# Banded attention with a bilinear FFN on one core: weighted sums of two head pairs moved, scores of a third joined to them, output banks in another order

## The chip, the core and the metric

The kernel runs on one core of one Trainium2 chip. Its engines work side by side and meet at semaphores: TensorE (PE; PEld is its weight load), VectorE (DVE), ScalarE (ACT), GpSimd (POOL) and SyncE (SP), which here only issues DMAs. The metric is the device time of one launch in microseconds (us), as a median over runs; lower is better.

## The reference

For 8 sequences (here "batches") of 576 tokens with 8 heads of 64:

```
scores = q k^T / 8 - slope[h] * |i - j|      (only 0 <= i - j < 128, elsewhere -1e9)
attn   = softmax(scores);  x = attn v         (x: 4608 tokens x 512)
out    = ((x w_a) * (x w_b)) w_out            (d_ff = 1536)
```

Inputs and output are f32. The kernel computes the large products in f16 with each operand split into a high and a low half (three matmuls for one product), so that PE does three times the plain number of matmuls.

## The kernel before

**Two streams on PE.** The main stream is the FFN: per batch an `up` phase (x times w_a and w_b, their product) and a `down` phase (times w_out). From batch 1 on, PE's order is the written order (`manual_schedule` for PE alone). ACT, DVE, POOL and SP are ordered by a planner that simulates the program: whatever is ready first in that simulation goes first, with ties by written order and by priority; `tc.issue_after(x)` keeps an instruction behind x. The order of each queue is then fixed, and each engine works through its own in turn.

**A step** of the main stream is six matmuls of 288 columns (function `terms`, or two f of `down`). For batches 4 to 6, `up` has 84 steps in two interleaved lanes (`up_fast`): each lane owns one `ch` bank, which ACT reads after its first, and third step (L1158, L1170) and DVE after its fifth and seventh (L1181, L1193); the lane's `p` steps use one of the two side banks ef0 and ef1 (read at L1165, L1176, L1186). The next use of a bank waits for that read. Batches 1 to 3 do all, six or two of the twelve f in a plainer way (`up_plain`, read at L1084 and L1086).

**The side stream** is the attention of the next batches, generator `attention()`. It goes pair by pair (two heads, p = 0 to 3 in a batch). `weave` and `Pace` set how far it may go: its values `yield i + v/7` are places, and one pair takes 24 steps of a `down` or 42 of an `up`. During `up` of batch b it is at pairs p = 2 and p = 3 of the batch b + 1; during `down` at p = 0 and p = 1 of the batch after. The parts of a pair are:

- `score_pair(o, 0)`, `score_pair(o, 1)`: 64x64 matmuls of q and k into two banks each, then DVE's bias and minimum (L508) and ACT's exponential (L509); the second bank's DVE and ACT work is a function `rest` that is called later.
- `normalize`: probabilities in f16, high half by ACT (L547), low half by DVE (L548), into the one buffer `packed` (tile phl).
- `transpose_probs`: one DMA transpose on SP's queue from `packed` into the one buffer pT (L558).
- `split_v`: v in two f16 halves (vhl, two buffers). `pv_phase(0)`, `pv_phase(1)`: 36 and 30 to 36 matmuls of 64x64 that form x; between them DVE reads one column (`mid`, L677), after them ACT copies x out (`keep_x`, L567) and squares it.
- `split` and `lay_out`: q and k of the next pair in two halves (`qkh` by ACT L459, `qkl` by DVE L464) and copied across partitions (tile qst, one buffer, four DMAs on SP); `load`: the DMAs of the pair after (one buffer qk, free after L464).

Score and x banks, and two small sums, come in turn from a ring of four banks (place "at"). The pair p = 1 is not transposed in its own turn: its transpose and its products with v come in p = 2, behind those of p = 0 (held in `late`).

**Banks of the main stream.** `places["bank"]` is an endless cycle over ef0, ef1 and the two `ch` buffers; `up_plain` takes four an f, `down` takes eight a batch (dn_ps, read at L1243) and `hidden_scale` two. The cycle goes on from batch to batch without a restart.

Of the kernel before, what the change touches and what calls it, by code (L numbers as in the profile page):

```python
# [88 lines left out]
def attention_then_bilinear_ffn(ctx: ExitStack, tc: tile.TileContext, qT, kT, vP, w_a, w_b, w_out, rel, slopes2, outT):  # L89
# [12 lines left out]
    def share_banks():  # L102

        places["ef"] = three[:2]
        places["bank"] = cycle(three[:2] + ((ps_ch, "ch"),) * 2)
        places["at"] = cycle(((ps_at, "at"),) * 3 + three[2:])

# [733 lines left out]
    def attention():  # L841
# [36 lines left out]
        for i in range(n + 1):  # L878
# [6 lines left out]
            if p == 3 and b > 1:  # L885
                pv_phase(1, late.p, st, late)
                transpose_probs(prev)
            if two == 2:
                rest = score_pair(o, 0, nxt.ready if p == 1 and nxt else None)
                yield i + 0.5 / 7  # L890
                rest()
            elif o:
                scores(o, 0)
# [18 lines left out]
            if p == 2 and b > 1:  # L912
                pv_phase(0, late.p, st, late)
                split(nxt)
            elif p == 2:
                pv(late.p, st, late, late.vhl)
                transpose_probs(prev)
                split(nxt)
# [5 lines left out]
            if p == 0 and prev and prev.b > 1:  # L924
                yield i + 2.3 / 7
                pv_phase(0, prev.p, st, prev)
            yield i + 3 / 7
            if two == 2:
# [3 lines left out]
                elif p == 3:  # L932
                    pv_phase(0, prev.p, st, prev)
                    yield i + 3.7 / 7
                if p == 0 and prev.b > 1 or p == 3:
                    pv_phase(1, prev.p, st, prev)
                elif p == 2:
                    pv_phase(1, late.p, st, late)
                    transpose_probs(prev)
                rest = score_pair(o, 1)  # L940
                yield i + (3.5 if p in (1, 2) or p == 0 and prev.b > 1 else 4.2 if p == 3 else 4) / 7
# [3 lines left out]
                yield i + (4.2 if p == 3 else 4) / 7  # L945
# [27 lines left out]
            if o:  # L973
                with behind():
                    normalize(o)
            if p == 0 and b == 1:
# [8 lines left out]
            if p == 2 and b > 1:  # L985
                pv_phase(0, prev.p, st, prev)
            elif p == 2:
                pv(prev.p, st, prev, prev.vhl)
            if p == 1 or p == 2 and b > 1:
                late = prev  # L990
            elif o:
                transpose_probs(o)
            prev, o = o, nxt
# [392 lines left out]
    def batch(b):  # L1386
# [10 lines left out]
        weave(att.along(up(states[b], h, plain, fast, seven), n_up, NPAIR * b + 4), *sides[0])  # L1397
        if seven:
# [10 lines left out]
    share_banks()  # L1409
    with tc.manual_schedule(engines={mybir.EngineType.PE}):  # L1410
# [42 lines left out]
```

## Time and profile before

| | |
|---|---|
| median of 3 runs | 989.89 us (988.83 to 992.11) |
| profiled execution | 988.87 us, span 987.1 us, granted clock 0.998 of full |
| PE busy | 945.2 us (96%), 10312 matmuls |
| DVE, ACT, POOL busy | 721.7 us (73%), 636.0 us (64%), 261.0 us (26%) |

A busy PE is a modelled figure: a matmul of 288 columns is shown as 286 ns, though the next one starts 0.12 us after it. Where PE is fed, a step therefore starts 0.73 to 0.74 us after the step before; a later start is a loss, a little larger than the idle time that a row shows.

### The profile page before, as it was taken

The numbers are of one execution on the slowest core, as the hardware profiler recorded it, in microseconds if no ns is written. First come the engines' busy times: TensorE is split into PE (matmuls) and PEld (weight loads), VectorE is DVE, ScalarE is ACT, GpSimd is POOL, SyncE is SP. The second block draws the span as 40 slices with busy tenths as digits, with TensorE's granted clock in tenths as the row PEclk, the third lists the DMA queues.
The fourth block names the chain that finished last, engine by engine and source line by source line (L and its number), as shares of the span: only waits on it lengthen the run. The fifth ranks groups of instructions, "written<-read, shape, count | busy, mean of one in ns | idle before, by whom it ended". The sixth has DMA issues, their size and how long they took to land.

```text
span 987.1 us, 25870 instructions
## 1 busy us (share of the span) xinstructions
PE 945.2 (96%) x10312; PEld 732.2 (74%) x10313; DVE 721.7 (73%) x2028; ACT 636.0 (64%) x1725; POOL 261.0 (26%) x307
## 2 busy tenths in 40 slices
PE   8989999989989999998999999999899999999998
PEld 6657777767767777776777777777677777777776
DVE  6999997577878758766886676767677685589860
ACT  6878788576676667766766766767567765434531
POOL 1211132045455123640533012321134012221110
PEclk9999999999999999999999999999999999999999
DMA  9372845513335232453135342363314521200001
GB/s 343 136 270 95 268 92 127 150 37 75 73 88 149 50 46 56 101 144 72 37 72 136 75 72 42 81 151 75 78 42 92 149 48 37 42 31 13 1 7 43
DMA packets 136152, 91.15 MB, mean 92 GB/s; under 512 B 101600, under 2 KB 122208, under 8 KB 135008
## 3 DMA queue, kind: packets, MB, share of 16 engines
q1 hardware_dynamic: 126528, 79.97, 33.0%
q10 hardware_dynamic: 9504, 9.54, 3.0%
q8 instruction: 80, 1.31, 0.6%
q14 instruction: 40, 0.33, 0.1%
HBM read 48.33 MB, written 9.44 MB: 59 GB/s over the span
## 4 chain that ended last, share of the span: by engine, by line
PE 59%; DVE 12%; ACT 12%; DMA 11%; issue 3%; POOL 2%; SPq 1%; ACTq 0%; DVEq 0%; POOLq 0%
PE ch L1073 13%; PE up_ps L1073 12%; PE p L1073 10%; PE dn_ps L1238 10%; DMA pT<-phl 6%; PE x_ps L674 3%; PE dn_ps L1035 2%; ACT t L509 2%; DMA qk<-in_kT 2%; DVE t L508 2%; DMA v<-in_vP 2%; PE dch L1263 2%; ACT phl L547 2%; DVE xr L589 2%; PE d L1263 1%
## 5 line engine op out<-in xcount | busy, mean ns | idle before, releaser
L1073 PEld LDWEIGHTS <-wup 128*128 128x128 f16 x3072 | 295.7, 98 | 101.5 <-issue 26.1
L1238 PE MATMUL dn_ps<-h,wdn 128*128 128x288 f16 x1728 | 218.9, 286 | 2.9 <-DVE row L1186 1.1
L1073 PE MATMUL up_ps<-xr,wup 128*128 128x288 f16 x1536 | 197.2, 286 | 8.2 <-ACT xr L1084 4.6
L1238 PEld LDWEIGHTS <-wdn 128*128 128x128 f16 x1728 | 165.7, 98 | 47.4 <-issue 3.5
L1073 PEld LDWEIGHTS <-wsum 128*128 128x128 f16 x1152 | 111.5, 98 | 39.1 <-issue 10.0
L1188 POOL TENSOR_TENSOR xr<-xr,row 128x288 f32<-128x288 f32 x64 | 60.0, 938 | 299.4 <-DVE row L1186 272.4
L509 ACT ACTIVATE t<-t,mn 128x192 f32<-128x192 f32 (+2 forms) x252 | 107.5, 431 | 29.6 <-DVE mn L508 29.6
L1073 PE MATMUL ch<-xr,wup 128*128 128x288 f16 x768 | 115.0, 286 | 9.2 <-DVE xr L1193 7.4
L1073 PE MATMUL ch<-xr,wsum 128*128 128x288 f16 x768 | 111.3, 286 | 7.7 <-ACT xr L1158 7.6
L1073 PE MATMUL p<-xr,wup 128*128 128x288 f16 x768 | 115.1, 286 | 0.4 <-ACT xr L1176 0.4
L548 DVE SCALAR_TENSOR_TENSOR phl<-t,rin,phl 128x192 f16<-128x192 f32 (+2 forms) x252 | 100.5, 444 | 15.5 <-ACT phl L547 14.6
L547 ACT ACTIVATE phl<-t,rin 128x192 f16<-128x192 f32 (+2 forms) x252 | 89.2, 429 | 26.2 <-DMA pT<-phl 13.1
L1065 ACT CAST h<-xr 128x576 f16<-128x576 f32 x84 | 56.2, 669 | 49.2 <-DVE xr L1086 18.5
L508 DVE CUSTOM_DVE_ANT_0 t<-sc_ps,bias,neg 128x192 f32<-128x192 f32 (+2 forms) x216 | 73.3, 390 | 9.8 <-PE sc_ps L525 9.6
L1066 DVE TENSOR_TENSOR h<-xr,h 128x576 f16<-128x576 f32 x78 | 60.8, 779 | 25.8 <-ACT h L1065 24.8
L589 DVE TENSOR_TENSOR xr<-v,xr 128x576 f16<-128x576 f32 x52 | 49.8, 968 | 26.7 <-ACT xr L588 26.4
L483 POOL TENSOR_SCALAR bias<-rel_sb,ninv,sl_sb 128x192 f32<-128x192 f32 x24 | 26.9, 1122 | 152.9 <-DVE mn L508 125.7
L1170 ACT ACTIVATE row<-ch,g 128x288 f32<-128x288 f32 x64 | 31.8, 497 | 52.6 <-PE ch L1073 51.1
L1073 PE MATMUL p<-xr,wsum 128*128 128x288 f16 x384 | 57.6, 286 | 0.1
L588 ACT CAST xr<-v 128x576 f16<-128x576 f32 x52 | 34.9, 673 | 21.3 <-POOL v L607 16.6
L509 ACT ACTIVATION_READ_ACCUMULATOR t<-t,mn 128x1 f32 x252 | 48.5, 193 | 0.0
L583 POOL TENSOR_TENSOR xq<-xq,sq 128x576 bf16<-128x576 bf16 x21 | 30.7, 1462 | 53.0 <-ACT sq L582 52.8
(200 smaller groups left out, 1553.4 us busy)
## 6 DMA issues: line engine op xcount, KB each, us to landing
v<-in_vP SPq DMA_DIRECT2D x8, 1280.0 KB, 6.2
qk<-in_qT SPq DMA_DIRECT2D x28, 288.0 KB, 3.9
qk<-in_kT SPq DMA_DIRECT2D x28, 288.0 KB, 4.6
out<-row ACTq DMA_DIRECT2D x56, 144.0 KB, 2.2
wdn<-in_w_a SPq DMA_DIRECT2D x12, 512.0 KB, 5.0
wdn<-in_w_b SPq DMA_DIRECT2D x12, 512.0 KB, 6.0
wdn<-in_w_out SPq DMA_DIRECT2D x12, 512.0 KB, 6.0
qst<-qkh SPq DMA_DIRECT2D x24, 80.0 KB, 2.3
```

The costliest lines, as they stand in the source:

```text
L508: beside[1] = vec.tensor_tensor_reduce(out=t[:, c:c + w], in0=ps[:, c:c + w], in1=o.bias[:, WIN - w:WIN], scale=-0.125 if o.b == 1 else o. ...
L509: beside[0] = act.activation(t[:, c:c + w], t[:, c:c + w], AF.Exp, bias=o.mn[:, n:n + 1], scale=-1.0, accum_out=o.sm[:, n:n + 1])
L547: beside[0] = last_phl[0] = act.activation(to[:, 0, pc:pc + w], e, AF.Copy, scale=s)
L548: beside[1] = vec.scalar_tensor_tensor(out=to[:, 1, pc:pc + w], in0=e, scalar=s, in1=to[:, 0, pc:pc + w], op0=ALU.mult, op1=ALU.subtract)
L588: act.copy(xs[:, n, 0, :, :], src)
L589: vec.tensor_tensor(out=xs[:, n, 1, :, :], in0=src, in1=xs[:, n, 0, :, :], op=ALU.subtract)
L1065: act.copy(h[:, f, :, 0, :], hid)
L1066: eng.tensor_tensor(out=h[:, f, :, 1, :], in0=hid, in1=h[:, f, :, 0, :], op=ALU.subtract)
L1073: pe.matmul(ps[:, 0:HT], w[:, wi, k, :], xs[:, b, xi, k, :], start=(first and n == 0), stop=(last and n == len(ks) - 1), skip_group_check= ...
L1170: last_read[0] = last_main[0] = act.activation(mid, ch, AF.Copy, scale=st.g)
L1188: pool.tensor_tensor(out=x0, in0=x0, in1=mid, op=ALU.mult)
L1238: pe.matmul(ps[:, 0:HT], wdn[:, f, wi, e * P:(e + 1) * P], h[:, f, t, hi, :], start=(m == 0 and n == 0), stop=(m == NF - 1 and n == 2))
```

## The change

It has four parts. In pair p = 2 (`b > 1`) the second half of the products of pair 0 with v, the transpose of pair 1 and the second scores come at place 2.5/7 in place of 3/7, and the second scores' `rest` at 3/7 in place of 3.5/7. The products of pair 1 with v come at 5.5/7 and 6/7 of p = 2, in place of 6/7 and of the start of p = 3; the transpose of pair 2 and the first scores of pair 3 follow them at 6/7, so the first scores of p = 3 leave the start of p = 3 and only their `rest` stays there, without the half place between. In p = 3 the products of pair 2 with v come at 2.3/7 and 3/7 (before 3/7 and 3.7/7), the second scores with them, their `rest` at 3.5/7 (before 4.2/7). Last, the cycle of banks is restarted before every `down`, in the order side bank, `ch`, other side bank, `ch`, with the first side bank by the number of fast f.

```diff
     def share_banks():
         places["ef"] = three[:2]
-        places["bank"] = cycle(three[:2] + ((ps_ch, "ch"),) * 2)
         places["at"] = cycle(((ps_at, "at"),) * 3 + three[2:])
+
+    def down_banks(n):
+
+        a = max(n, 1) % 2
+        places["bank"] = cycle((three[a], (ps_ch, "ch"), three[1 - a], (ps_ch, "ch")))
...
             if p == 3 and b > 1:
-                pv_phase(1, late.p, st, late)
-                transpose_probs(prev)
-            if two == 2:
+                rest()
+            elif two == 2:
                 rest = score_pair(o, 0, nxt.ready if p == 1 and nxt else None)
                 yield i + 0.5 / 7
                 rest()
...
             if p == 2 and b > 1:
                 pv_phase(0, late.p, st, late)
                 split(nxt)
+                yield i + 2.5 / 7
+                pv_phase(1, late.p, st, late)
+                transpose_probs(prev)
+                rest = score_pair(o, 1)
             elif p == 2:
...
-            if p == 0 and prev and prev.b > 1:
+            if prev and prev.b > 1 and p in (0, 3):
                 yield i + 2.3 / 7
                 pv_phase(0, prev.p, st, prev)
             yield i + 3 / 7
@@
-                elif p == 3:
-                    pv_phase(0, prev.p, st, prev)
-                    yield i + 3.7 / 7
-                if p == 0 and prev.b > 1 or p == 3:
+                elif p in (0, 3):
                     pv_phase(1, prev.p, st, prev)
-                elif p == 2:
-                    pv_phase(1, late.p, st, late)
-                    transpose_probs(prev)
-                rest = score_pair(o, 1)
-                yield i + (3.5 if p in (1, 2) or p == 0 and prev.b > 1 else 4.2 if p == 3 else 4) / 7
+                if p != 2:
+                    rest = score_pair(o, 1)
+                    yield i + (4 if p == 0 and prev.b == 1 else 3.5) / 7
                 rest()
                 if p == 3 and nxt:
                     low_qk(nxt, beside[1])
-                yield i + (4.2 if p == 3 else 4) / 7
+                yield i + 4 / 7
...
+            if p == 2 and b > 1:
+                yield i + 5.5 / 7
+                pv_phase(0, prev.p, st, prev)
...
             if p == 2 and b > 1:
-                pv_phase(0, prev.p, st, prev)
+                pv_phase(1, prev.p, st, prev)
             elif p == 2:
                 pv(prev.p, st, prev, prev.vhl)
-            if p == 1 or p == 2 and b > 1:
+            if p == 1:
                 late = prev
             elif o:
                 transpose_probs(o)
+            if p == 2 and b > 1:
+                rest = score_pair(nxt, 0)
             prev, o = o, nxt
             yield i + 1
...
         weave(att.along(up(states[b], h, plain, fast, seven), n_up, NPAIR * b + 4), *sides[0])
+        down_banks(len(fast) // 2)
         if seven:
...
     share_banks()
+    down_banks(0)
     with tc.manual_schedule(engines={mybir.EngineType.PE}):
```

## Rows read from the trace of the kernel before

**Rows 1.** The page's chain that ended last, by line, share of the span.

```profile
PE ch L1073 13%; PE up_ps L1073 12%; PE p L1073 10%; PE dn_ps L1238 10%; DMA pT<-phl 6%; PE x_ps L674 3%; PE dn_ps L1035 2%; ACT t L509 2%; DMA qk<-in_kT 2%; DVE t L508 2%; DMA v<-in_vP 2%; PE dch L1263 2%; ACT phl L547 2%; DVE xr L589 2%; PE d L1263 1%
```

**Rows 2.** Waits of PE, whole span: us in total, times, longest us.

```profile
PE ch L1073 <- ACT xr L1158: 7.6, 9, 2.3
PE ch L1073 <- DVE xr L1193: 7.4, 9, 2.0
PE up_ps L1073 <- ACT xr L1084: 4.6, 4, 1.8
...
PE ch L1073 <- ACT row L1170: 1.9, 2, 1.2
...
PE sc_ps L525 <- ACT v L567: 1.4, 3, 0.7
...
PE dn_ps L1238 <- DVE row L1186: 1.1, 1, 1.1
```

**Rows 3.** PE in time, batch 4: start, us, line, tiles, count, idle before and releaser.

```profile
579.70 0.90 PE L1073 MATMUL ch<-xr,wsum 128*128 128x288 f16 x6
582.49 0.90 PE L1073 MATMUL ch<-xr,wsum 128*128 128x288 f16 x6 [1.89 <-ACT xr L1158]
```

**Rows 4.** ACT in time, batch 4, ahead of that start.

```profile
577.56 0.67 ACT L1065 CAST h<-xr 128x576 f16<-128x576 f32 x1 [0.31 <-DVE xr L1193]
580.48 1.68 ACT L547 ACTIVATE phl<-t,rin 128x192 f16<-128x192 f32 x5 [2.24 <-DMA pT<-phl]
582.06 0.38 ACT L1158 COPY xr<-ch 128x288 f32<-128x288 f32 x1
```

**Rows 5.** Waits of ACT on that transfer, 280 to 860 us.

```profile
ACT phl L547 <- DMA pT<-phl: 13.1, 6, 3.1
```

**Rows 6.** PE's waits of this kind in batch 6 (782 to 854 us).

```profile
PE ch L1073 <- ACT xr L1158: 0.4, 1, 0.4
```

**Rows 7.** SP's queue in time: batch 2, then batch 4.

```profile
342.09 3.91 SPq L558 DMA_TRANSPOSE pT<-phl  x1
...
571.04 0.60 SPq L431 DMA_DIRECT2D qk<-in_qT  x1
...
572.39 5.18 SPq L558 DMA_TRANSPOSE pT<-phl  x1
```

**Rows 8.** ACT in time, batch 2: the wait after the first of these transposes.

```profile
348.89 1.68 ACT L547 ACTIVATE phl<-t,rin 128x192 f16<-128x192 f32 x5 [1.37 <-DMA pT<-phl]
```

**Rows 9.** PE in time, batch 4, start of pair 3.

```profile
597.23 0.90 PE L1073 MATMUL ch<-xr,wup 128*128 128x288 f16 x6 [0.77 <-DVE xr L1193]
597.96 0.90 PE L1073 MATMUL p<-xr,wup 128*128 128x288 f16 x6
...
601.18 0.65 PE L1073 MATMUL ch<-xr,wsum 128*128 128x288 f16 x4 [0.85 <-ACT xr L1158]
```

**Rows 10.** ACT in time, batch 4, before and at the start of pair 3.

```profile
587.83 0.50 ACT L1170 ACTIVATE row<-ch,g 128x288 f32<-128x288 f32 x1 [1.28 <-PE ch L1073]
...
598.72 1.17 ACT L442 ACTIVATE qkl<-qk 128x1152 bf16<-128x1152 f32 x1
...
600.75 0.38 ACT L1158 COPY xr<-ch 128x288 f32<-128x288 f32 x1
```

**Rows 11.** PE in time, batch 4: the second scores of pair 2.

```profile
570.58 0.69 PE L674 MATMUL x_ps<-pT,vhl 64*64 64x128 f16 x30
...
571.72 0.27 PE L525 MATMUL sc_ps<-qkh,qst 64*64 64x192 f16 x2 [0.36 <-ACT v L567]
```

**Rows 12.** ACT in time around those scores.

```profile
568.31 1.26 ACT L459 ACTIVATE qkh<-qk,own 128x1152 f16<-128x1152 f32 x1 [0.90 <-DVE own L457]
...
571.23 0.71 ACT L567 ACTIVATE v<-x_ps 128x320 f32<-128x320 f32 x2
```

**Rows 13.** PE in time, from up to down of batch 3.

```profile
512.35 0.90 PE L1073 MATMUL ch<-xr,wsum 128*128 128x288 f16 x6
514.37 0.65 PE L1238 MATMUL dn_ps<-h,wdn 128*128 128x288 f16 x4 [1.12 <-DVE row L1186]
```

## The prediction

> **What bounds the kernel now.** I read the busy table first: PE is busy 96% of the span, so only what PE loses can be won. Then the chain that ended last [rows 1]: its long links are PE's own steps, but one DMA stands among them, the transpose into pT, with 6% of the span. Then PE's waits [rows 2]: the two largest kinds are a `ch` bank that ACT (L1158, 7.6 us in 9 waits) or DVE (L1193, 7.4 us in 9) has not yet read. Last, I followed PE's steps in time, batch by batch. The `down` phases from batch 2 on run without a wait of note; the losses sit in the `up` phases, where pairs 2 and 3 are worked in. There the same few places recur, and the change touches four of them. A loss is counted from start to start: a step takes 0.735 us when it is fed (597.23 to 597.96, [rows 9]), so the step of [rows 3] that starts at 579.70 should be followed at 580.44, is followed at 582.49, and loses 2.05 us where the row shows 1.89 us of idle time. I add 0.16 us to each wait for that.
>
> **What does not change.** No matmul, ACT, DVE or DMA instruction is added or removed. A stretch of 64x64 matmuls between main steps has a switch in and out; there are seven such stretches in an `up` before, at steps 1, 13, 19, 37, 43, 61 and 65 of 84 (place v/7 comes after step 6v, rounded down, plus 1; 42 more for pair 3), and seven after, at steps 1, 13, 16, 34, 37, 56 and 61. So that part costs nothing, because the first scores of pair 3 go along with the products they stood beside before. PE's order is written out; the orders on ACT, DVE and SP are the planner's, and that is where the doubt lies.
>
> **A, the banks.** At the end of `up` of batch 3 the first dn_ps lies in the side bank whose last reader is the last but one step of the later lane: it starts at 514.37 in place of 512.35 + 0.735 = 513.09 and loses 1.28 us [rows 13]. With five fast pairs of f the new cycle begins with ef1, which the earlier lane left some steps before. In batches 4 to 6 the cycle happened to begin well, and in batch 1 the order is a ring of four as before, so nothing is won there. Between 0 (something else is late there) and 1.3, I take -1.2 us.
>
> **B, the transpose of pair 1.** This is the largest term. In pair 2, ACT's first probability op (L547) must wait until the transpose has read `packed`; it waits 2.24 us until 580.48, and L1158 stands behind it on ACT's queue until 582.06 [rows 4]. PE's step waits for just that read [rows 3]. So 2.05 us of PE are lost to a transfer. ACT has six such waits, 13.1 us together [rows 5]: five lie at this place (batches 2 to 6), the sixth in a `down`, where PE does not feel it. PE's losses by it are 2.3 + 0.16 in batch 5, 2.0 + 0.16 in batch 3 (the longest of the two kinds, [rows 2]; there the late read is DVE's, which waits for ACT), 2.05 in batch 4, 0.4 + 0.16 in batch 6 [rows 6], about nothing in batch 2 (plain steps, more slack). Sum 7.2 us. The transpose waits for the last product of pair 0; with these three steps sooner it can be issued 3 x 0.735 = 2.2 us sooner, against waits of 1.4 to 3 us [rows 5, 8]. The `rest` of the second scores comes three steps sooner too, so ACT arrives a little sooner, which eats some of that. Bounds: 0, if SP issues it no sooner (below), and -7.2; I take -6.0.
>
> A rule bears on this term. On SP the transpose stands behind the two loads of q and k (571.04 first, transpose 572.39, [rows 7]) and is 8.1 us from issue to ACT's release (580.48, [rows 4]); in batch 2 without loads just ahead it is 342.09 to 348.89, 6.8 us [rows 7, 8]. If the transpose now goes first, I count 6.8 us. The Trainium skill, "DMA: Bandwidth & Descriptors", section "Issuing engines are not separate DMA queues", says that all DMAs run on the same 16 DMA engines and interleave, so that loads issued right behind would stretch the transpose as loads ahead of it do. The two rows agree with some stretch; by the rule the term would be some 1.3 us smaller in each of batches 3 to 5, so -2.1 in place of -6.0.
>
> **C, the start of pair 3.** Before, ACT and DVE get there at once the x copies of pair 1, v's halves, five minima and exponentials and the squares of the next pair: L1158 runs at 600.75, behind the squares at 598.72 [rows 10], and PE loses 0.77 + 0.16 and 0.85 + 0.16 us within six steps [rows 9]. There are seven such losses: two each in batches 4 and 5, one each in batches 2, 3 and 6; with 0.93 to 1.02 us each, 6.7 us. After the change the products and the first three minima fall at step 37, where ACT had idle time (1.28 us before L1170 at 587.83, [rows 10]), and only `rest` and the squares stay at step 43. The work is the same, spread over six more steps. Not all of it is won, since after step 37 a lane's L1193 follows just as it did after step 43, one step later. Bounds 0 and -6.7; I take -4.0.
>
> **D, the second scores behind the x copies.** The ring of four banks gives the second scores' second bank the place of the first x bank, so PE waits in the middle of a stretch: 571.72 for L567, which starts at 571.23 [rows 11, 12]. There are three such waits, 0.7 us longest [rows 2]; with the start to start loss 2.1 us. At the new place, three steps after the first products and the small sum for the next pair, ACT's qkh (L459, 568.31 to 569.57) is just under way when the products end at about 569.1 (570.58 + 0.69 - 3 x 0.735). L567 then starts at about 569.6, the bank is free at 570.0, and PE loses 1.05 us, in batches 3 to 6, with 0.5 in batch 2: 4.7 in place of 2.1. Bounds: 0 more (L567 goes before qkh), and 2.2 more in each of five batches if L567 starts no sooner than today; I take +2.6.
>
> **E, a denser ACT after it.** qkh (1.26), the x copies (0.71), then exponentials now fall into the three steps in which the lanes' own reads were alone. No row of before has that crowd at this step; the nearest is C's, 0.93 to 1.02 us lost for a crowd. From nothing to 1.0 in each of five batches, I take half: +2.5. The wait for `mid` between the two halves of products has now three steps in place of six; a read of one column with 2.2 us of room costs nothing unless DVE is that far behind. Waits of the plain batches (L1084, 4.6 us, [rows 2]) lie mostly in the early steps of pair 2, which don't move: 0.
>
> **Sum.** -1.2 - 6.0 - 4.0 + 2.6 + 2.5 = -6.1 us. Against the profiled execution of 988.87 us that is 982.8; the median of the runs is 1.0 us above that execution, so I predict 983.7 us for the median.
>
> **The rivals.**
>
> 1. *The transpose goes no sooner.* The planner issues SP's queue in its own order; the loads wait for L464, the last reader of their one buffer, and today start at 571.04 [rows 7], beside the products' end (570.58 + 0.69, [rows 11]). If it still puts them ahead of the transpose, the transpose is issued at 572.4 as before, and B is 0. For: the loads stand first today. Against: L464 does not move, so they would be ready some 2 us after the products now. The sum is -1.2 - 4.0 + 2.6 + 2.5 = -0.1: 989.8 us, no change.
>
> 2. *Slower: the second scores wait the three steps out.* Place: the second score bank in pair 2 of batches 2 to 6; price: 2.2 us each, as L567 starts no sooner than today because qkh and the lanes' reads go first on ACT; 11 us in place of the 2.6 of D. With the other terms, -1.2 - 6.0 - 4.0 + 11 + 2.5 = +2.3: 992.2 us. It decides from about 1.8 us per batch on. For: qkh is ready exactly then [rows 12]. Against: today L567 starts as the products end [rows 11, 12], so nothing keeps it back for long. The Trainium skill, "TensorEngine Tiling (Array Packing)", section "PSUM Bottleneck", says that tiling speeds up TensorE but not the reading of PSUM, which may become the bottleneck; that is this rival in general words, and the wait of [rows 11] is a small case of it.
>
> 3. *More is won.* L567 goes before qkh and nothing crowds: D and E are 0, and B and C come whole: -1.2 - 7.2 - 6.7 = -15.1, 974.8; with some of C left, about 977.5 us.
>
> **How the numbers follow.** About 0.3% (3 us) is what a measurement of this kernel can tell from no change. Forecast 0.55, with 979 to 987.5 as its own range; rival 1 0.18; rival 2 0.12; rival 3 0.15. Faster by over 0.3% (below 986.9): 0.52 of the forecast, rival 3, and 0.02 of rival 1: 0.69. Within: 0.03 + 0.14 + 0.03 = 0.20. Slower (above 992.9): 0.02 + 0.09 = 0.11. Range 977 to 991: it leaves out the upper part of rival 2 and the lower of rival 3, under 0.2 together.
>
> **What would show it.** B: in batches 3 to 5 the transpose of pair 1 is issued before the loads, ACT's wait for it is under 0.5 us, and PE's start 30 steps into `up` has no wait. C: the two waits at the start of pair 3 are gone or under half. D: a wait for L567 of about 1 us in the stretch at step 16 of batches 3 to 6. A: the first dn_ps of batch 3 without a wait. The prediction is wrong if ACT's waits for the transpose stay above 1.5 us, or if PE's waits in the `up` phases of batches 2 to 6 fall by less than 3 us or by more than 10.

## The result, and the profile after

The changed kernel takes 975.25 us (median of 4 runs, 973.54 to 976.59) against 990.07 (988.83 to 992.11) for the kernel before beside it: ratio 0.9847, 95% interval 0.9824 to 0.9870. It is faster by 14.8 us, 2.4 times the 6.1 us forecast, and 1.75 us below the low end of the range. The profiled execution took 974.88 us, 14.0 less than that of before.

The head of the page, the busy table (us, share, instructions) and the chain that ended last, after:

```profile
span 972.9 us, 25898 instructions
PE 941.9 (97%) x10312; PEld 731.2 (75%) x10313; DVE 724.9 (75%) x2028; ACT 635.7 (65%) x1725; POOL 263.4 (27%) x307
PE ch L1080 15%; PE dn_ps L1245 14%; PE up_ps L1080 13%; PE p L1080 11%; DMA pT<-phl 3%; PE x_ps L678 2%; PE dch L1270 2%; DVE phl L552 2%; PE sc_ps L529 2%; PE dn_ps L1042 1%; DVE xr L593 1%; PE d L1270 1%; DMA qk<-in_kT 1%; ACT phl L551 1%; DMA v<-in_vP 1%
```

The lines moved by a few: L1073 is now L1080, L1158 L1165, L1193 L1200, L567 L571, L558 L562. PE's and DVE's counts are those of before: no work went. On the chain the transposes' share went from 6% [rows 1] to 3%.

PE's waits in `up` of batch 4, before and then after (us in total, times, longest us):

```profile
PE ch L1073 <- ACT xr L1158: 3.3, 3, 1.9
PE ch L1073 <- DVE xr L1193: 0.8, 1, 0.8
PE sc_ps L525 <- ACT v L567: 0.4, 1, 0.4
```

```profile
PE sc_ps L529 <- ACT v L571: 1.4, 1, 1.4
```

With 0.16 us for each wait, as the prediction counts, that is 4.5 + 5 x 0.16 = 5.3 us before and 1.56 after: 3.7 us less. The same stage as a window, before and then after (from:to, us, busy time of PE, PEld, DVE, ACT and POOL with counts, granted clock, DMA share, GB/s):

```profile
554.17:628.66 74.49, 70.05 (x819) 54.41 (x817) 52.49 (x149) 49.73 (x131) 17.32 (x16) 1.00 0.33 65
```

```profile
547.08:617.82 70.74, 69.30 (x818) 54.43 (x816) 52.45 (x148) 49.28 (x131) 17.83 (x16) 1.00 0.30 66
```

The stage is 3.75 us shorter, so in batch 4 the lost waits are all of the gain. The same reading for every `up`, stage lengths from the windows and waits with 0.16 us added to each:

| `up` of batch | 1 | 2 | 3 | 4 | 5 | 6 |
|---|---|---|---|---|---|---|
| before, us | 84.23 | 77.89 | 79.33 | 74.49 | 74.16 | 70.90 |
| after, us | 85.77 | 76.96 | 72.69 | 70.74 | 70.56 | 71.13 |
| PE's waits before | | 4.0 | 9.1 | 5.3 | 5.0 | 2.1 |
| PE's waits after | | 2.8 | 1.7 | 1.6 | 1.5 | 2.0 |

Batches 2 to 6 gain 14.7 us, and their waits fell by 15.9; `up` of batch 1 loses 1.5, its `down` gains 0.6; the other `down` stages keep their 39.80 us (37.07 in batch 6). That is 13.8 of the 14.0 us. One stage of one execution is good to about 1 us: a second trace of the same kernel (`e17_whole`) has 71.64 us in batch 4 and 85.10 in batch 1, and nearly the same sum over all stages (686.69 against 686.79).

Where PE waited 1.89 us for ACT in batch 4 [rows 3], it now runs through, a step each 0.73 us:

```profile
569.29 0.90 PE L1080 MATMUL ch<-xr,wsum 128*128 128x288 f16 x6
570.02 0.90 PE L1080 MATMUL ch<-xr,wup 128*128 128x288 f16 x6
```

ACT's first probability op there has no wait for the transpose any more; the 0.26 us left are DVE's:

```profile
570.25 1.68 ACT L551 ACTIVATE phl<-t,rin 128x192 f16<-128x192 f32 x5 [0.26 <-DVE rin L547]
572.43 0.40 ACT L1165 COPY xr<-ch 128x288 f32<-128x288 f32 x1
```

On SP the transpose of batch 4 now stands first and the loads 6.7 us behind it, the other way round than in [rows 7]:

```profile
561.34 3.85 SPq L562 DMA_TRANSPOSE pT<-phl  x1
...
568.04 0.62 SPq L435 DMA_DIRECT2D qk<-in_qT  x1
```

The second scores pay for it, as forecast; PE in batch 4:

```profile
560.60 0.69 PE L678 MATMUL x_ps<-pT,vhl 64*64 64x128 f16 x30
...
562.78 0.27 PE L529 MATMUL sc_ps<-qkh,qst 64*64 64x192 f16 x2 [1.40 <-ACT v L571]
```

Batch 2 pays too, by the transfer itself. There one load has slipped in ahead of the transpose, which takes 4.73 us on SP; ACT waits 3.94 us for it, then does nine probability ops before the read that PE waits for. SP, ACT and PE:

```profile
337.93 0.59 SPq L435 DMA_DIRECT2D qk<-in_qT  x1
338.63 4.73 SPq L562 DMA_TRANSPOSE pT<-phl  x1
```

```profile
346.72 3.06 ACT L551 ACTIVATE phl<-t,rin 128x192 f16<-128x192 f32 x9 [3.94 <-DMA pT<-phl]
349.68 0.38 ACT L1091 COPY xr<-up_ps 128x288 f32<-128x288 f32 x1
```

```profile
350.11 1.14 PE L1080 MATMUL up_ps<-xr,wup 128*128 128x288 f16 x8 [2.08 <-ACT xr L1091]
```

And the step from `up` to `down` of batch 3 [rows 13] is closed:

```profile
506.55 0.90 PE L1080 MATMUL ch<-xr,wsum 128*128 128x288 f16 x6
507.28 0.90 PE L1245 MATMUL dn_ps<-h,wdn 128*128 128x288 f16 x6
```

### The profile page after: what moved, and what is told of

Read it like the earlier page. It is cut to its first block, busy times and chain, and to the rows that moved or that the text cites. A ratio compares the mean times of both kernels' runs of the same rounds, so it can differ in the third digit from the quotient of the medians.

```text
span 972.9 us, 25898 instructions
## 1 busy us (share of the span) xinstructions
PE 941.9 (97%) x10312; PEld 731.2 (75%) x10313; DVE 724.9 (75%) x2028; ACT 635.7 (65%) x1725; POOL 263.4 (27%) x307
## 4 chain that ended last, share of the span: by engine, by line
PE 64%; DVE 15%; ACT 8%; DMA 8%; issue 3%; POOL 1%; SPq 1%; ACTq 0%; DVEq 0%
PE ch L1080 15%; PE dn_ps L1245 14%; PE up_ps L1080 13%; PE p L1080 11%; DMA pT<-phl 3%; PE x_ps L678 2%; PE dch L1270 2%; DVE phl L552 2%; PE sc_ps L529 2%; PE dn_ps L1042 1%; DVE xr L593 1%; PE d L1270 1%; DMA qk<-in_kT 1%; ACT phl L551 1%; DMA v<-in_vP 1%
## 5 line engine op out<-in xcount | busy, mean ns | idle before, releaser
L1080 PEld LDWEIGHTS <-wup 128*128 128x128 f16 x3072 | 295.5, 98 | 93.8 <-issue 18.3
L1080 PE MATMUL up_ps<-xr,wup 128*128 128x288 f16 x1536 | 197.0, 286 | 9.5 <-ACT xr L1091 5.7
L1080 PEld LDWEIGHTS <-wsum 128*128 128x128 f16 x1152 | 111.7, 98 | 32.4 <-issue 3.5
L1195 POOL TENSOR_TENSOR xr<-xr,row 128x288 f32<-128x288 f32 x64 | 63.1, 986 | 247.6 <-DVE row L1193 206.3
L1080 PE MATMUL ch<-xr,wup 128*128 128x288 f16 x768 | 115.0, 286 | 1.3 <-ACT row L1177 0.9
L1080 PE MATMUL p<-xr,wup 128*128 128x288 f16 x768 | 115.2, 286 | 0.2 <-ACT xr L1183 0.2
L1080 PE MATMUL ch<-xr,wsum 128*128 128x288 f16 x768 | 111.6, 286 | 1.6 <-ACT xr L1165 1.2
L1073 DVE TENSOR_TENSOR h<-xr,h 128x576 f16<-128x576 f32 x78 | 63.3, 812 | 27.6 <-ACT h L1072 27.0
L1080 PE MATMUL p<-xr,wsum 128*128 128x288 f16 x384 | 57.6, 286 | 0.0
```

What stands on the lines that cost most here:

```text
L1073: eng.tensor_tensor(out=h[:, f, :, 1, :], in0=hid, in1=h[:, f, :, 0, :], op=ALU.subtract)
L1080: pe.matmul(ps[:, 0:HT], w[:, wi, k, :], xs[:, b, xi, k, :], start=(first and n == 0), stop=(last and n == len(ks) - 1), skip_group_check= ...
L1195: pool.tensor_tensor(out=x0, in0=x0, in1=mid, op=ALU.mult)
```

## The experiments

The change has four separable parts: the new bank cycle, and three moves. The *first move* brings the second half of pair 0's products, the transpose of pair 1 and the second scores in pair 2 from 3/7 to 2.5/7. The *second* works off pair 1's products at 5.5/7 and the end of pair 2 with the transpose and the first scores of pair 3. The *third* brings pair 2's products in pair 3 from 3/7 and 3.7/7 to 2.3/7 and 3/7.

### Each part alone

The kernel before, with one part: the new cycle (`e1_banks`), the first move (`e3_pair0`), the second (`e4_pair1`), the third (`e5_pair2`).

```
# e1_banks
+    def down_banks(n):
+        a = max(n, 1) % 2
+        places["bank"] = cycle((three[a], (ps_ch, "ch"), three[1 - a], (ps_ch, "ch")))
# e3_pair0
             if p == 2 and b > 1:
                 pv_phase(0, late.p, st, late)
                 split(nxt)
+                yield i + 2.5 / 7
+                pv_phase(1, late.p, st, late)
+                transpose_probs(prev)
+                rest = score_pair(o, 1)
# e4_pair1
+            if p == 2 and b > 1:
+                yield i + 5.5 / 7
+                pv_phase(0, prev.p, st, prev)
...
-                pv_phase(0, prev.p, st, prev)
+                pv_phase(1, prev.p, st, prev)
...
+                rest = score_pair(nxt, 0)
# e5_pair2
-            if p == 0 and prev and prev.b > 1:
+            if prev and prev.b > 1 and p in (0, 3):
                 yield i + 2.3 / 7
                 pv_phase(0, prev.p, st, prev)
```

> Only the new cycle of output banks, attention as before. Theory (the gain is a sum of separate waits, each part of the change takes away its own): the first dn_ps of batch 3 no longer waits, 1.3 us less; with it perhaps the two up_ps waits of batch 3 near step 9 (1.9 us), which are also gone after the whole change, so 1.3 to 3.2 us less, 987 to 989. Rival (the parts only work together, because ACT's and DVE's load is spread by all of them at once): under 1 us. If the banks matter more than the trace of before shows: over 4 us.

> Only the first move: second products of pair 0, transpose of pair 1 and second scores of pair 2 at 2.5/7, their rest at 3/7; old banks, all else as before. Theory (separate waits): ACT's wait for the transpose in the up phases of batches 2 to 6 goes (10 us before), with it PE's waits near step 31 to 41 (8.5 us in batches 3 to 6); the second scores wait longer for the x copies (1.7 us more), a few us come anew; 4 to 7 us less, 983 to 986. The waits at the start of pair 3 (6.7 us) stay. Rival (only together): less than 3 us, as the waits move to the next crowded place. Rival (transpose unimportant): ACT's wait goes, PE's time stays.

> Only the second move: products of pair 1 at 5.5/7 and 6/7 of pair 2, the transpose of pair 2 and the first scores of pair 3 with them; the products of pair 0 and the banks as before. Theory (separate waits): the seven waits at the start of pair 3 go (6.7 us), those near step 31 (7 to 8 us) stay: 4 to 6.7 us less, 983 to 986. Rival (only together): with the transpose of pair 1 as late as before, pT and the probabilities come too late for step 34 to 37, PE waits there, and less than 2 us is won or it is slower.

> Only the third move: in pair 3 the products of pair 2 at 2.3/7 and 3/7, the second scores with them, their rest at 3.5/7; all else as before. Theory (separate waits): few waits lie there (1.4 us in batch 2, 0.7 in batch 3, 0.2 in batches 4 and 5): 0 to 2 us less, 988 to 990. Rival (only together): no change or slower by up to 2 us, as the products then stand right behind the crowded start of pair 3.

| kernel | median us | ratio to before | 95% interval |
|---|---|---|---|
| e1_banks | 991.06 | 0.9993 | 0.9976 to 1.001 |
| e3_pair0 | 989.11 | 0.9976 | 0.9960 to 0.9991 |
| e4_pair1 | 987.57 | 0.9961 | 0.9941 to 0.9980 |
| e5_pair2 | 986.72 | 0.9943 | 0.9924 to 0.9963 |

The new cycle shortens `up` of batch 3 by 1.7 us (79.33 to 77.65), and its total can't be told from no change. The first move takes away the wait 30 steps into `up`, but alone it gives back part of that: in batch 4 the second scores wait 1.4 us, 1.0 more than before, and batches 1 and 2 become 2.2 and 1.4 us longer. The other waits of batch 4, at steps 8, 46 and 50, lie elsewhere and stay. PE's waits in `up` of batch 4 with the first move alone, then with the second alone:

```profile
PE ch L1102 <- ACT xr L1187: 1.4, 2, 0.8
PE sc_ps L534 <- ACT v L576: 1.4, 1, 1.4
PE ch L1102 <- DVE xr L1222: 0.8, 1, 0.8
```

```profile
PE ch L1102 <- ACT xr L1187: 2.3, 2, 1.9
PE sc_ps L534 <- ACT v L576: 0.4, 1, 0.4
```

The second move takes away the waits at the start of pair 3 (in all batches, seven of seven) and leaves those of the transpose; it also makes `up` of batch 1 2.0 us longer, with a new wait of 2.2 us for `mid`. So B and C are two causes, each with its own part of the change. The third move, which had no term, has the best median, though its interval overlaps that of the second. Its traced execution shows less (2.6 us by stages); part of that gap is the kernel before itself, whose runs beside this one have a median of 991.84 us while the execution shown here took 988.87. The next group settles its size.

### Each move left out of the whole

```
# e14_less_pair2
-            if prev and prev.b > 1 and p in (0, 3):
+            if p == 0 and prev and prev.b > 1:
                 yield i + 2.3 / 7
                 pv_phase(0, prev.p, st, prev)
# e15_less_pair1
-            if p == 2 and b > 1:
-                yield i + 5.5 / 7
-                pv_phase(0, prev.p, st, prev)
# e16_less_pair0
-                yield i + 2.5 / 7
-                pv_phase(1, late.p, st, late)
-                transpose_probs(prev)
-                rest = score_pair(o, 1)
# e2_no_banks
-    down_banks(0)
```

> The whole change less its third move (pair 2's products in pair 3 at 3/7 and 3.7/7 as before). The prediction gave this move nothing; alone it won 0.57% (0.37 to 0.76), of which the stages of its trace show only 2.6 us. Theory (the parts add up, and this one is worth what its trace shows): 2 to 3 us slower than the whole change. Rival (it is worth what its median showed): 5 to 6 us slower. Rival (worth nothing, as predicted): within 1 us.

> The whole change less its second move (products of pair 1, transpose of pair 2 and first scores of pair 3 at their old places). Theory (the parts add up): the seven waits at the start of pair 3 come back, 5 to 7 us slower than the whole change. Rival (interaction: with the first move made, ACT is ahead and the crowd at the start of pair 3 does less): 2 to 4 us slower.

> The whole change less its first move (second products of pair 0, transpose of pair 1 and second scores of pair 2 at 3/7 as before). Theory (the parts add up): PE's waits near step 31 come back in batches 3 to 6 (7 to 8 us with the wait for the transpose), the longer waits for the x copies and those of batch 2 go (3 us): 3 to 6 us slower than the whole change. Rival (interaction: the products of pair 1 at step 34 meet a transpose that lands just then): over 7 us slower.

> The whole change once more, on the chip of these runs, so that the three others are read against it: ratio 0.983 to 0.986 to the kernel before.

> The whole change without the new cycle of output banks (the old cycle that goes on from batch to batch). Theory: only the wait of the first dn_ps of batch 3 comes back, 1.3 to 1.6 us slower than the whole change. Rival (the banks also removed the up_ps waits of batch 3 near step 9): 3 us slower or more.

| kernel | median us | ratio to before | 95% interval | sum of `up` and `down`, us |
|---|---|---|---|---|
| e17_whole | 976.47 | 0.9855 | 0.9839 to 0.9872 | 686.69 |
| e14_less_pair2 | 981.36 | 0.9898 | 0.9882 to 0.9914 | 691.00 |
| e15_less_pair1 | 983.60 | 0.9919 | 0.9907 to 0.9932 | 693.68 |
| e16_less_pair0 | 982.23 | 0.9917 | 0.9900 to 0.9933 | 691.20 |
| e2_no_banks | 977.90 | 0.9858 | 0.9835 to 0.9881 | 690.00 |

The first four ran on one chip, the last on another. Within the whole the third move is worth 4.3 us by stages (4.9 by the medians), the second 7.0 (7.1), the first 4.5 (5.8). Without the third, batch 2's wait of 1.23 us for DVE is back:

```profile
391.29 0.90 PE L1102 MATMUL ch<-xr,wup 128*128 128x288 f16 x6 [1.23 <-DVE xr L1222]
```

and `up` of batches 2 to 5 is longer by 1.0, 0.6, 0.45 to 1.35 and 0.2 to 0.5 us (against the two traces of the whole). The rest is batch 1, 1.1 to 2.0 us in its `up` and `down` together. Four waits of the kernel before go with this move, two at the end of pair 3 in batches 2 and 3 and two at the start of `down` of batch 1:

```profile
387.84 0.90 PE L1073 MATMUL ch<-xr,wup 128*128 128x288 f16 x6 [1.24 <-DVE xr L1193]
505.70 0.90 PE L1073 MATMUL ch<-xr,wup 128*128 128x288 f16 x6 [0.50 <-DVE xr L1193]
274.06 0.90 PE L1238 MATMUL dn_ps<-h,wdn 128*128 128x288 f16 x6 [0.90 <-ACT xr L1084]
280.02 1.14 PE L1238 MATMUL dn_ps<-h,wdn 128*128 128x288 f16 x8 [0.91 <-DVE h L1066]
```

With 0.16 us each they are 4.2 us. All four stand in the traces of every kernel without the third move (in `e14_less_pair2` 1.23, 0.49, 0.51 and 0.61 us); of the kernels with it, the first three stand in none and the fourth is at most 0.3 us.

Without the second, batch 4's two waits stand there again (0.8 us each), without the first the 2.0 us of the transpose:

```profile
PE sc_ps L534 <- ACT v L576: 1.4, 1, 1.4
PE ch L1102 <- ACT xr L1187: 0.8, 1, 0.8
PE ch L1102 <- DVE xr L1222: 0.8, 1, 0.8
```

```profile
PE ch L1102 <- ACT xr L1187: 2.3, 2, 2.0
PE sc_ps L534 <- ACT v L576: 0.4, 1, 0.4
```

The first two moves are worth more in the whole than alone, where the medians gave 2.7 and 4.3 us. The old bank cycle brings back the wait of 1.3 us (1.4 with the 0.16) at the end of `up` of batch 3 and can't be told apart from the whole in its ratio. Its stages show 3.2 us, but that trace is of the slowest of its five runs (980.27 us); another 1.1 to 1.8 us of them lie in `up` of batch 1.

### Is it the transpose's place on SP?

`e6_late_t` writes the transpose of pair 1 half a place later in the generator; `e10_t_behind_loads` keeps everything and has the loads of q and k issued ahead of it, as before; `e11_late_rest` keeps the transpose and puts the `rest` of the second scores back to 3.5/7.

```
# e6_late_t
                 pv_phase(1, late.p, st, late)
-                transpose_probs(prev)
                 rest = score_pair(o, 1)
...
+                if p == 2:
+                    transpose_probs(prev)
                 rest()
# e10_t_behind_loads
-                transpose_probs(prev)
+                behind_load = load(i + 2)
+                with tc.issue_after(behind_load.ins) if behind_load else ExitStack():
+                    transpose_probs(prev)
...
-            load(i + 2)
+            if not (p == 2 and b > 1):
+                load(i + 2)
# e11_late_rest
+                if p == 2:
+                    yield i + 3.5 / 7
                 rest()
```

> The whole change, but the transpose of pair 1 alone goes back from 2.5/7 to 3/7 of pair 2 (the products and scores stay early). Theory (PE lost to ACT's wait for this transfer): SP then has the loads of q and k ahead of it again or issues it 2 to 3 us later, ACT waits 1 to 3 us for it in batches 3 to 5, and PE's waits near step 31 come back with 1 to 2 us in each of two or three batches: 2 to 5 us slower than the whole change. Rival (the gain of the first move is the earlier rest, not the transfer): within 1 us of the whole change, ACT reaches the transfer's wait and PE does not feel it.

> The whole change, but in pair 2 the loads of the pair after are put ahead of the transpose of pair 1 on SP's queue (as in the kernel before); in the run with the transpose written later the planner issued it as early as ever, so that run told nothing. Theory (PE lost to ACT's wait for this transfer): the transpose is issued 3 us later, at 564.5 in place of 561.3, and lands about 572; ACT, which comes at 570.3 in batch 4, waits 1 to 3 us in each of batches 3 to 5, and PE's wait near step 31 comes back with 1 to 2.5 us each: 3 to 7 us slower than the whole change, 979 to 983 where that has 976. Rival (the earlier rest is what helps): ACT waits, PE does not feel it, within 1 us of the whole change.

> The whole change, but the rest of the second scores of pair 2 goes back from 3/7 to 3.5/7; products and transpose stay early. Theory (the transfer): the transpose still lands before ACT comes, so no wait near step 31 comes back; within 1 us of the whole change, or a little faster, as the crowd at step 20 is thinner. Rival (the earlier rest is what helps): 2 to 5 us slower, with PE's waits back near step 31.

`e6_late_t`: 976.60 us, 0.9857 (0.9833 to 0.9880). The planner issued the transpose right after the products all the same (SP at 562.99, 3.84 us), so this run says nothing on its place: the line where an operation is written isn't where SP gets it.

`e10_t_behind_loads`: 989.86 us, 0.9982 (0.9965 to 0.9999). Nearly the whole gain is gone, though the products, scores and banks stand where the change put them. SP, DVE, ACT and PE in batch 4:

```profile
572.97 0.60 SPq L440 DMA_DIRECT2D qk<-in_qT  x1
573.61 0.61 SPq L441 DMA_DIRECT2D qk<-in_kT  x1
574.32 5.24 SPq L567 DMA_TRANSPOSE pT<-phl  x1
```

```profile
571.53 1.42 DVE L473 SCALAR_TENSOR_TENSOR qkl<-qk,own,qkh 128x1152 f16<-128x1152 f32 x1 [0.26 <-ACT qkh L468]
```

```profile
582.77 0.98 ACT L556 ACTIVATE phl<-t,rin 128x192 f16<-128x192 f32 x3 [3.11 <-DMA pT<-phl]
```

```profile
584.09 0.90 PE L1105 MATMUL ch<-xr,wsum 128*128 128x288 f16 x6 [1.30 <-DVE xr L1213]
585.35 0.90 PE L1105 MATMUL ch<-xr,wsum 128*128 128x288 f16 x6 [0.36 <-ACT xr L1190]
```

The chain is whole in these lines. The products end at 571.00, but SP works through its queue in order, and its next entry is a load whose buffer DVE's qkl op (L473) reads until 572.95; two issues of 0.6 us follow, so the transpose goes 3.3 us after the products and takes 5.24 us on SP in place of 3.85. ACT waits 3.11 us for it; PE's steps behind wait 1.30 and 0.36. In batch 2 ACT waits 4.9 us and PE 3.01. By stages the `up` of batches 2 to 5 loses 4.2, 2.6, 2.6 and 2.4 us, which is all of the 11.6 us lost (698.39 against 686.79 us of `up` and `down`). Most of batch 2's 4.2 us is TensorE's clock: when PE goes on behind its wait of 3.01 us, at 353.98, it runs at half speed, 1.2 of 2.4 GHz (in the window line the sixth figure behind the length, 0.50, is the granted clock):

```profile
353.20:359.80 6.60, 5.82 (x25) 3.60 (x25) 3.17 (x8) 2.60 (x8) 0.00 (x0) 0.50 0.00 0
```

PE's 5.82 busy us there would be 2.9 at full clock, so by this estimate the transfer's place costs 8.7 us by itself and 2.9 us by the clock that fell behind the longest wait. ACT's waits for the transfers from 280 to 860 us come to 16.8 us in 6, against 13.1 in [rows 5] and 7.1 in 4 after the change:

```profile
ACT phl L556 <- DMA pT<-phl: 16.8, 6, 4.9
```

```profile
ACT phl L551 <- DMA pT<-phl: 7.1, 4, 3.9
```

So the exponentials that the moves bring forward are worth next to nothing unless the transpose comes forward too; with loads ahead they only arrive earlier at the same wait.

`e11_late_rest`: 977.05 us, 0.9849 (0.9825 to 0.9872), as the whole. It is the transfer and not the earlier `rest` that won.

### The price: is it the bank, and does the join matter?

`e7_no_join` leaves the first scores of pair 3 at the start of pair 3. `e8_own_bank` lets the small sum share a bank, so that the ring of four turns by one and the second scores need no bank of the x copies.

```
# e7_no_join
-            if p == 2 and b > 1:
-                rest = score_pair(nxt, 0)
...
             if p == 3 and b > 1:
+                rest = score_pair(o, 0)
+                yield i + 0.5 / 7
                 rest()
# e8_own_bank
-        tot = bank("vtot", "at")
+        tot = shared[0] = bank("vtot", "at")
...
-        tot = bank("qtot", "at")
+        tot = shared[0][:, 256:512] if p == 3 and b > 1 else bank("qtot", "at")
```

> The whole change, but the first scores of pair 3 stay at the start of pair 3 (own stretch at step 43 of 84, rest half a place later, as before). Theory (the start of pair 3 was crowded with ACT's and DVE's work of two things at once): the x copies and v halves are gone from there, so of the 6.7 us at most a third comes back, 1 to 2 us, with 0.1 us for the added stretch in each of six batches: 1 to 3 us slower than the whole change. Rival (the scores' work itself is the crowd): the waits at step 46 to 51 come back whole, 5 to 7 us slower.

> The whole change, and in pair 2 the small sum for the next pair is written to free columns of the small sum of v's bank, so that the ring of four turns one place less and the second scores no longer come to the first x bank. Theory: the waits of the second scores for the x copies in batches 2, 4 and 6 (3.8 us from start to start after the change) are gone, 2 to 4 us less than the whole change, 971 to 973. Rival (given back: ACT has the same queue to work off, so PE meets it two or three steps later at a ch bank, as in batch 5 where the wait is 1.0 us at step 20): less than 1.5 us won.

`e7_no_join`: 978.18 us, 0.9867 (0.9845 to 0.9888). By stages 1.3 us are lost (688.10 against 686.79): the main gain of the second move is the earlier products, not the join.

`e8_own_bank`: 976.93 us, 0.9856 (0.9832 to 0.9879), no gain. The waits of 1.4 us for the x copies in batches 4 and 6 are gone, and in both another stands four steps on, as one already did in batch 5 of the changed kernel (0.86 us); in batch 4, and the three together:

```profile
569.96 0.90 PE L1104 MATMUL ch<-xr,wup 128*128 128x288 f16 x6 [0.91 <-ACT row L1201]
```

```profile
PE ch L1104 <- ACT row L1201: 2.8, 3, 1.0
```

PE gets to the main steps sooner and finds the same ACT late there: of the 1.56 us lost in batch 4, 1.07 come back. So the bank named in the wait limited little of it, and ACT's queue most. By stages batches 4 and 6 are 0.6 and 0.5 us shorter; batch 2 is 1.8 us longer in this trace, about as much as a stretch at half clock there costs (354.0 to 357.3, granted clock 0.50).

### A better version

In early batches the moves cost time: alone, the first makes `up` of batches 1 and 2 longer and the second that of batch 1. `e12_by_batch` makes the first move only for the attention of batches 4 to 6 and the second only for 3 and later (a batch's attention runs in the `up` of the batch before). `e13_split_later` also puts `split(nxt)`, whose qkh op stands ahead of the x copies on ACT, half a place later where the first move is made.

```
# e12_by_batch
+            PAIR0, PAIR1 = b in range(4, 7), b in range(3, B)
# e13_split_later, with it
                 pv_phase(0, late.p, st, late)
-                split(nxt)
+                if not PAIR0:
+                    split(nxt)
...
+                if p == 2 and PAIR0:
+                    split(nxt)
                 rest()
```

> The whole change, but by batch of the attention: the first move (pair 0) for batches 4 to 6 alone and the second (pair 1) for batches 3 to 7. Theory (waits add up batch by batch): up of batch 1 gets its 1.8 us back, up of batch 2 loses its wait of 2.2 us near step 36 and its wait of 0.6 for the x copies, up of batch 6 gets 0.5 us back: 3 to 5 us less than the whole change, ratio 0.980 to 0.982 to the kernel before. Rival (each order is a new throw of the planner's): within 1.5 us of the whole change.

> As the run by batch, and in pair 2 of batches 4 to 6 the split of the next pair's q and k comes at 3/7, behind the second scores, so that ACT's qkh no longer stands ahead of the x copies. Theory: the second scores' wait of 1.6 us in batch 4 goes, and the wait of 1.0 us near step 20 in batch 5: 1 to 3 us less than the run by batch. Rival (ACT has the same work in the same steps and PE meets it later): within 1 us of it, with a wait near step 20 to 25 in its place.

`e12_by_batch`: 973.60 us (972.47 to 975.82), 0.9817 (0.9792 to 0.9841). `e13_split_later`: 971.12 us (970.40 to 972.15), 0.9790 (0.9766 to 0.9813); on the same chip `e11_late_rest`, equal to the whole change, ran 975.99 to 978.13. So `e13_split_later` beats both kernels, the changed one by about 0.6%. Its `up` of batch 1 is back at 83.83 us, and in batch 4 only this wait of PE is left, the one for the x copies being gone:

```profile
PE ch L1104 <- ACT row L1201: 0.3, 1, 0.3
```

That fits the reason given in D: it was qkh on ACT that kept the x copies late. Not all of it is won: `up` of batch 3 is 1.0 us longer than in `e12_by_batch` (73.68 against 72.70), with waits of 0.8 us for `mid` and 1.1 us for ACT near the start of pair 3.

## Why the prediction was too small

The places that the prediction named were right, most sizes fell short, and one part of the change had no term. Term by term, in PE's time and with 0.16 us per wait, from the two profiled executions (the profiled total fell by 14.0 us):

| term | forecast | measured | 
|---|---|---|
| A, banks | -1.2 | -1.3 |
| B, transpose of pair 1, batches 3 to 6 | -6.0 | -7.2 |
| the same transfer in batch 2 | 0 | +2.2 |
| C, start of pair 3 | -4.0 | -6.7 |
| D, second scores | +2.6 | +1.7 |
| E, crowd behind the second scores | +2.5 | +1.0 |
| third move, waits in batches 2 and 3 | 0 | -2.1 |
| batch 3, waits at steps 8, 10 and 41 | 0 | -3.2 |
| small waits elsewhere in `up` of 2 to 6 | 0 | -0.1 |
| `up` and `down` of batch 1 | 0 | +0.9 |
| sum | -6.1 | -14.8 |

The measured column sorts the waits of the table above by their place: A to C are those listed in the prediction, gone to the last one; D is 3.66 us less 1.92 (before, three waits of 1.44 us together, with the 0.16 less than the prediction's 2.1); E is one wait of 0.86 us in batch 5, at step 20, the only one in the steps right behind the second scores; the small waits are six of 0.2 to 0.5 us before and six after. The 0.8 us between -14.8 and the -14.0 of the profiled executions isn't laid to a place. Two slips of the prediction change little: 982.8 + 1.0 is 983.8 and not 983.7, and C's seven losses run from 0.87 us (batch 3), not from 0.93.

**The step that failed first** is the part that was never sized: the third move. The prediction works through A to E and has no sentence for pair 2's products in pair 3. Left out of the whole, it costs 4.3 to 4.9 us, and alone it gives 0.57% (0.37 to 0.76). The four waits shown with `e14_less_pair2` make 4.2 us of it: the table's 2.1, and 2.1 in batch 1, where the losses by the first two moves hide it. Their releasers are DVE and ACT; which of their operations came sooner was not followed.

The second thing without a term is batch 3. The prediction says of the plain waits "lie mostly in the early steps of pair 2, which don't move: 0". In `up` of batch 3 they did go: 1.3 us for L1084 at step 8, 0.25 right behind it, and 1.15 us for L1170 at step 41. The waits of this stage before (the second of the two for L1170, 0.7 us, is C's):

```profile
PE ch L1073 <- ACT row L1170: 1.9, 2, 1.2
PE up_ps L1073 <- ACT xr L1084: 1.3, 1, 1.3
```

The early steps don't move, but what ACT still has to do when they come does. The wait at step 8 goes with the first move alone, and without it when the other two are made together (`e16_less_pair0`). The one at step 41 falls from 1.15 us to 0.57 with the first move alone and to 0.34 with the second alone, and is gone with both.

**C** failed by a cut without a row: "Not all of it is won, since after step 37 a lane's L1193 follows just as it did after step 43". All seven waits went, with the second move alone too (`e4_pair1`). The same work spread over six more steps left the lanes' reads on time.

**B** was right in its chain for batches 3 to 6, and there its cut of 1.2 us came to nothing. All its checks hold: transpose ahead of the loads, no wait at the step, ACT's wait below 0.5 us in batches 3 to 5. For batch 2, "about nothing", it was wrong: one load stands ahead of the transpose there, and PE loses 2.2 us. The doubt in B's rival, that the planner might keep the loads first, was the right one to have: `e10_t_behind_loads` is that rival made true, and measured 989.86 us where the rival gave 989.8. The totals agree partly by luck: the transfer's place was worth 11.6 us and not B's 7.2, since batch 2 loses 4.2 us by it, most of that by the clock, and the other terms were too small by about as much. The Trainium skill, "DMA: Bandwidth & Descriptors", section "Issuing engines are not separate DMA queues", says that transfers interleave on the same 16 DMA engines, which by the prediction's estimate would have cut B to -2.1. The case did not come up here: the loads follow 6.7 us behind, past the small transfers to qst, and the transposes' median from issue to landing fell from 6.7 to 5.9 us over all 24. That loads just ahead are bad shows in `e10_t_behind_loads` (5.24 us on SP against 3.85) and in batch 2 (4.73).

**D** was right in place and reason: 1.40 us of idle time in batches 4 and 6, 0.4 in batch 2, none in 3 and 5, where I had 1.05 in each. Rival 2, which made it 2.2 us in five batches, is out. `e8_own_bank` adds what the prediction missed: another bank gets only a third of that time back.

**E** was too large as a crowd: of the five batches only batch 5 has a wait there, 1.0 us in place of 2.5 in all. Its side remark on `mid`, which "costs nothing unless DVE is that far behind", met that case in `up` of batch 1, where the second move's halves stand two steps apart and PE waits 1.13 us:

```profile
242.28 0.67 PE L678 MATMUL x_ps<-pT,vhl 64*64 64x128 f16 x28 [1.13 <-DVE mid L681]
```

That wait and batch 2's 2.08 us are both gone in `e12_by_batch`.

Rival 3 (974.8, "about 977.5") comes nearest, for other reasons: it had D and E at nothing, while D, E and the transfer in batch 2 came to 4.9 us, and what paid for them was the third move and batch 3. The bound named for a wrong prediction, that PE's waits in these stages fall by more than 10 us, was passed: they fell by 13.5 us of idle time.

## What to carry to other kernels

Give each hunk of a change its own term, and cut a term below the sum of its waits only with a row that says what keeps them: here the hunk without a term and the two cuts without a row were some 8 us (4.3 + 1.2 + 2.7). A DMA queue that is worked through in order, as SP's is in `e10_t_behind_loads`, is part of the critical path as soon as a compute engine waits for one of its transfers; put the transfer that is waited for ahead of loads that have time, and of loads whose buffer isn't free yet, and check in the queue's own timeline that it went there. Before a wait for a bank is removed, see whether the engine that frees the bank is itself late: in `e8_own_bank` two thirds of the wait came back four steps on. And before two traces are compared by stages, look at the granted clock of each stage.

## What was not expected of the hardware

Two load issues of 0.6 us each ahead of one transpose per batch cost the kernel 11.6 us by stages. In batch 4 these are 2.0 us in which SP stands waiting for the loads' buffer, 1.3 us of its time for the issues, 1.4 us more for the transpose itself on SP (5.24 against 3.85 us), and the wait passed on through ACT.

TensorE's clock fell behind some of PE's waits of 2 us and more, and not behind others. It stood at half (1.2 of 2.4 GHz, granted clock 0.50) behind waits of 2.08 us (`e1_banks`, 696.6 to 699.8 us), 2.34 (`e4_pair1`, 695.5 to 698.8), 2.52 (`e8_own_bank`, 354.0 to 357.3) and the 3.01 of `e10_t_behind_loads`. Behind the 2.60 us of `e5_pair2`, the 2.29 of the kernel before (both batch 5) and the 2.08 of the changed one (batch 2) it stayed full. In the first three PE was busy all through these 3.2 to 3.3 us, so each of those stages is an estimated 1.6 us longer by it. So a wait of 2 us can cost more than its length.

Over all 24 transposes of this shape a change in what surrounds them shifts the median on SP from 4.28 to 3.95 us, before and then after (duration in ns, least, median and most):

```profile
L558 SPq DMA_TRANSPOSE pT<-phl x24: 3782/4280/5905, 183.3 to 849.9; - x24
```

```profile
L562 SPq DMA_TRANSPOSE pT<-phl x24: 3823/3951/6007, 183.9 to 835.7; - x24
DMA to landing us min/median/max: 5.7/5.9/8.8
```
